# Two order changes in a gated attention and state-space kernel: g products ahead of q products, and the copies of the output stage's first two pairs of chunks

## The chip, the cores and the metric

The kernel runs on one core of one Trainium2 chip. The metric is device time in microseconds (us) for one execution, from 2048 input rows of 448 numbers to 2048 output rows of 448 numbers. Before the change the median of three runs was 168.16 us. The engines are named as the profile names them: PE multiplies matrices, PEld is its weight load, DVE and ACT are the two elementwise engines that can read PE's results, POOL is a third elementwise engine that works on on-chip memory only, SP and POOL issue the transfers.

## The reference

The output is `g*a + (1-g)*b`. `a` is linear attention with 16 heads of 28, `b` is a state-space convolution, `g` is one gate per row.

```python
phi = lambda t: jnp.where(t > 0, t + 1, jnp.exp(t)) + 1e-6
pq, pk = phi(q), phi(k)                       # q, k, v = x @ wqkv, split in heads
kv = jnp.einsum("bhsd,bhse->bhde", pk, v)
z = jnp.einsum("bhsd->bhd", pk)
num = jnp.einsum("bhqd,bhde->bhqe", pq, kv)
den = jnp.einsum("bhqd,bhd->bhq", pq, z)[..., None] + 1e-6
a = (num / den).transpose(0, 2, 1, 3).reshape(B, S, D) @ wo
g = _sigmoid((x * gate_w).sum(-1, keepdims=True))
y = jnp.fft.irfft(jnp.fft.rfft(u_t, 2 * L) * Kf[None], 2 * L)[:, :, :L]
b = y.transpose(0, 2, 1) + u * D_skip
out = g * a + (1 - g) * b
```

## The kernel before

The 2048 rows are 16 chunks of 128. Products need about full precision from a fast matmul type, so every operand is split in a high and a low part, and a product of two operands is three matmuls (high with high, low with high, high with low). A "product" below is one of these matmuls.

**First stage, the loop over chunks (times about 24 to 112 us).** For each chunk PE runs three groups in turn. `project` makes 11 products of 448 columns for the keys of the next chunk (tile `k`, or a tile named `v` in every other chunk), then 11 products of 450 columns for the queries of this chunk (tile `q`; the two extra columns are the gate). `do_g` then makes 11 products of 448 columns that add `x^T phi(k)` into four accumulators `g0` to `g3`: three each for `g0`, `g1`, `g2`, and two for `g3`, the first of which loads only 64 columns of weights. So 22 products, 11 of `g` and 11 of `k`, lie between two runs of `q`. In two places there is more between them: four small transposes (tile `p`, line 319) within chunk 5's `g`, and two products (line 449) after chunk 12's. While PE does this, ACT and DVE turn `k` and `q` into features and split them, POOL makes low parts and products for `b`, and transfers bring the next chunk of `x`.

The work on each engine stands in the order in which the program was written (`manual_schedule`); no scheduler moves it. A framework adds the waits between engines. It counts two reads of one PE result tile by different engines as a conflict as well, and lets the later one in the program wait for the earlier.

**Middle stage (about 112 to 121 us).** From the copies `gs` of the four accumulators PE makes the key-value blocks (line 755), ACT and DVE mask and split them, and PE multiplies them with `wo` to a combined matrix of four blocks (`m_products`, line 735; split by `m_high` on ACT, line 739, and `m_low` on DVE, line 743). The last chunk's `q` run is spread over this stage in pieces (`q_run`), to fill PE's waits.

**Output stage (about 117 to 163 us).** For a pair of chunks (even, odd) the steps are: `norm_a` (POOL, line 596) multiplies the query features with the key sums, `norm_b` (DVE reduction, line 601) sums them per head, `norm_d` (DVE, lines 605 and 607, and a copy to on-chip memory on ACT, line 610) makes the reciprocal, `norm_c` (POOL lines 621 and 628, DVE line 624) scales the features. `turn_pe` (PE, line 633) transposes them: four transposes for an even chunk, the last of which holds pieces of both chunks, and three for an odd one. `turn_even` copies the even chunk's result, high part on ACT (line 640), low part on DVE (line 641); `turn_odd` does the same for the odd chunk (ACT line 652, DVE line 659) with four small copies on ACT from the even chunk's result (`odd_ends`, line 656). `attend` (PE, line 676) makes 11 products of 448 columns for one chunk; its first takes a high part, its second a low part. `final_b` (DVE line 681) and `final_c` (ACT line 687) empty its result.

A pair's `attend` products are issued one chunk late: `turn_pe` of chunks 2 and 3 comes ahead of `attend(1)`, and `attend(2)` follows it.

Of the kernel before, what the change touches and what calls it, by code (L numbers as in the profile page):

```python
# [7 lines left out]
F32 = mybir.dt.float32  # L8
# [3 lines left out]
ALU = mybir.AluOpType  # L12
# [10 lines left out]
J = 4  # L23
# [11 lines left out]
PADS = 32  # L35
G = 4
ROWS = {6: (0, 1), 7: (2, 3, 4), 8: (5, 6, 7), 9: (8, 9, 10), 10: (11, 12, 13), 11: (14, 15)}
SMALL = 2.0 ** -70
FLAT = 2.0 ** 35
BIG = 3.4028234e38  # L40
# [102 lines left out]
def gated_mix_kernel(ctx: ExitStack, tc: tile.TileContext, xin, wq_d, wvo_d, abc_d, ldt_d, dsk_d,  # L143
                     turn_d, cst_d, first_d, gin_d, out):
    nc = tc.nc
    PE, ACT, DVE, POOL, SP = nc.tensor, nc.scalar, nc.vector, nc.gpsimd, nc.sync
# [62 lines left out]
    o = 0  # L209
    for part in PARTS:  # L210
# [8 lines left out]
        o = e  # L219
# [124 lines left out]
    def project(*args, **kw):  # L344
        o, run = pieces(*args, **kw)
        run(11)
        return o
# [57 lines left out]
    gp = gps.enter_context(tc.tile_pool(name="gp", bufs=1, space=PSUM))  # L405
    g = [gp.tile([P, 512], F32, name="g%d" % i, tag="g%d" % i) for i in range(4)]

    def do_g(c, blocks=range(4)):
        w = xn[c]
        for i in blocks:  # L410
            a = w[:, 64 + i * P:64 + (i + 1) * P]
            b = w[:, XC - NAT + 64 + i * P:][:, :P] if i < 3 else None
            seq = [(a, pkh[c]), (a, pkl[c]), (b, pkh[c])] if i < 3 else \
                  [(a, pkh[c]), (a[:, :64], pkl[c])][::1 if c == 0 else -1]
            for n, (a, b) in enumerate(seq):
                PE.matmul(g[i][:a.shape[1], :D], lhsT=a, rhs=b, start=c == 0 and n == 0,  # L416
                          stop=c == NC - 1 and n == len(seq) - 1)

# [7 lines left out]
    def home(c):  # L426
        return homes[c // (2 * G)][:, c % (2 * G)]

    def running(c):
        if not c:  # L430
            sums.append(ps.tile([P, 512], F32, name="r", tag="v0")[:, :D])
            ACT.copy(sums[0], home(0))
        else:
            DVE.tensor_tensor(out=sums[0], in0=home(c), in1=sums[0], op=ALU.add)
        DVE.tensor_tensor(out=home(c), in0=near, in1=sums[0], op=ALU.mult)
# [82 lines left out]
    for c in range(2, NC - 2):  # L518
        if c + 3 < NC:
            load_x(c + 3)  # L520
        if c == 2:
            SP.dma_start(out=mask, in_=cst_d)
        if c in (6, 7):
            half_load(1, c - 6)
        if c == 10:
            for j in (0, 2):
                SP.dma_start(out=wo[:, j:j + 2], in_=wvo_d[:DJ, 1, j:j + 2])
        if c == 12:
            for j in (0, 2):
                SP.dma_start(out=wv[:, j:j + 2], in_=wvo_d[:, 0, j:j + 2])  # L530
        ko = project(c + 1, wkh, wkl, D, "v1" if c in (2, 4) or c > 6 and c % 2 == 0 else "k")
        rows = list(ROWS.get(c, ()))
        if c > 6 and rows:
            running(rows.pop(0))
        if c == 13:
            under(room[:, G:G + 2])
            under(room[:, G + 2:])
        split_t(c + 2)
        if c == 13:
            ACT.copy(over, sums[0])  # L540
            head_add(0)
            head_add(1)
        if c > 5:
            split_n(c + 2, False)
        k_feature(c + 1, ko)
        if c in (8, 9, 11):
            group_add((c - 7) * 2 // 3)
        if c == 12:
            whole_split()
        if c > 5:  # L550
            skip(c + 2)
        k_high(c + 1)
        k_low(c + 1)
        if rows:
            running(rows.pop(0))
        qo = project(c, wqh, wql, D + 2, "q")
        q_post(c, qo)
        for i in rows:
            running(i)
        if c < 5:  # L560
            steps(2 if c == 4 else 1)
        if c == 4:
            ACT.copy(tri, trir)
        if c == 7:
            SP.dma_start(out=okr[:, None, :DJ], in_=oks[:, None, :])
        if c == 9:
            DVE.tensor_reduce(out=okr[:, DJ:], in_=okr[:, :DJ], op=ALU.add, axis=AX.X)
            DVE.tensor_copy(okn, okr[:, DJ:])
        do_g(c, (0, 1))
        if c == 5:  # L570
            steps(1)
        do_g(c, (2, 3))
        if c < 4:
            skip(c - 1)
            skip(c + 2)
        if c < 6:
            split_n(c + 2, c > 3)
        if c in (3, 4):
            half_load(0, c - 3)
        for j in {11: (0, 1), 12: (2, 3)}.get(c, ()):  # L580
            split_o(j)
        if c == 12:
            whole_head()
        if c == 13:
            group_add(3)
            under(y[:, 2 * G:2 * G + 2])
            under(y[:, 2 * G + 2:3 * G])
# [4 lines left out]
    pn, th, tl, pd, dn, dp = {}, {}, {}, {}, {}, []  # L592
# [10 lines left out]
    def norm_d(c, n, copy=DVE.tensor_copy):  # L603
        r = dp[0][:, c:c + n]
        DVE.scalar_tensor_tensor(out=r, in0=r, scalar=1e-6, in1=e1[:, c:c + n, None].to_broadcast([P, n, H]),
                                 op0=ALU.add, op1=ALU.mult)
        DVE.reciprocal(out=r, in_=r)
        if c % 2 == 0:
            dn[c // 2] = tp.tile([P, 4, H], F32, name="den", tag="den", bufs=3)
        copy(dn[c // 2][:, c % 2:c % 2 + n], r)  # L610
# [19 lines left out]
    def turn_pe(c):  # L630
        o = p3.tile([P, 512], F32, name="tr", tag="tr")
        for j in range(4 - c % 2):
            PE.transpose(o[:, j * P:(j + 1) * P], pn[c][:, j], ident)  # L633
        return o

    def turn_even(c, o):
        t = xt_p.tile([P, 2, J, P], F32R, name="th", tag="t")
        th[c], tl[c] = t[:, 0], t[:, 1]
        ov = o.rearrange("p (j t) -> p j t", j=J)
        ACT.copy(th[c], ov)  # L640
        DVE.tensor_tensor(out=tl[c], in0=ov, in1=th[c].bitcast(F32), op=ALU.subtract)  # L641

    def turn_odd(c, o, oe):
        odd_high(c, o)
        odd_ends(c, 0, oe)
        odd_ends(c, 1, oe)
        odd_low(c, o)

    def odd_high(c, o):
        t = xt_p.tile([P, 2, J, P], F32R, name="th", tag="t")  # L650
        th[c], tl[c] = t[:, 0], t[:, 1]
        ACT.copy(th[c][:, :3], o[:, :3 * P].rearrange("p (j t) -> p j t", j=3))

    def odd_ends(c, i, oe):
        for half in (slice(0, DT), slice(DT, P)):
            ACT.copy((th, tl)[i][c][half, 3], oe[i * DT:(i + 1) * DT, 3 * P:])  # L656

    def odd_low(c, o):
        DVE.tensor_tensor(out=tl[c][:, :3], in0=o[:, :3 * P].rearrange("p (j t) -> p j t", j=3),
                          in1=th[c][:, :3].bitcast(F32), op=ALU.subtract)  # L660
# [17 lines left out]
    def final_b(c):  # L678
        ot = tp.tile([P, D], F32, name="ot", tag="pkh")
        for a, lo, hi in av[c]:  # L680
            DVE.scalar_tensor_tensor(out=ot[:, lo:hi], in0=y[:, c, lo:hi], scalar=og[:, c:c + 1],  # L681
                                     in1=a[:, lo:hi], op0=ALU.mult, op1=ALU.add)
            (ACT if c == NC - 1 and hi == D else SP).dma_start(out=oview[c, :, lo:hi], in_=ot[:, lo:hi])
# [5 lines left out]
    c = NC - 2  # L689
# [7 lines left out]
    k_low(c + 1)  # L697
    zh = tp.tile([P, D], F32R, name="zh", tag="w")
    zl = tp.tile([P, D], F32R, name="zl", tag="v0", bufs=1)
    qo = project(c, wqh, wql, D + 2, "q")  # L700
    do_g(c, (0, 1, 2))
    zo = ps.tile([P, 512], F32, name="zo", tag="v0")
# [13 lines left out]
    for i in range(4):  # L716
        do_g(c + 1, (i,))
        ACT.copy(gs[i], g[i][:, :D])
        if i == 1:
            qo, q_run = pieces(c + 1, wqh, wql, D + 2, "q")  # L720
# [17 lines left out]
    def m_high(j, o):  # L738
        ACT.copy(mh[:DJ, j] if j < 3 else shl[:, 0], o[:DJ, :D])
# [34 lines left out]
    def kv_low(r, o):  # L774
        DVE.tensor_tensor(out=kvl[:, 2 * r:2 * r + 2], in0=o, in1=kvh[:, 2 * r:2 * r + 2].bitcast(F32), op=ALU.subtract)

    q_run(1)
    k1 = kv_products(1)
    k0 = kv_products(0)
    k1 = kv_split(1, k1)  # L780
# [16 lines left out]
    t0 = turn_pe(0)  # L797
    t1 = turn_pe(1)
    q_run(2)
    norm_a(4)  # L800
    turn_even(0, t0)
    odd_high(1, t1)
    norm_b(2)
    norm_b(3)
# [2 lines left out]
    o1 = m_products(1, ps, "v0")  # L807
    m_high(0, o0)
    m_high(1, o1)
    ACT.copy(mh[:DT, 3], shl[:DT, 0].bitcast(F32))  # L810
    odd_ends(1, 0, t0)
    norm_d(2, 2, ACT.copy)
    ACT.copy(low_w3[0][:DT], shl[:DT, 0].bitcast(F32))
    m_low(0, o0)
    m_low(1, o1)
# [25 lines left out]
    norm_b(4)  # L841
    norm_a(7)
    norm_b(5)
    norm_d(4, 2, ACT.copy)
    for c in range(2, NC, 2):
        more = c + 2 < NC
        final_b(c - 2)
        t0 = turn_pe(c)
        t1 = turn_pe(c + 1)
        if more:  # L850
            norm_c(c + 2)
        if c + 6 < NC:
            norm_a(c + 6)
        if c + 4 < NC:
            norm_b(c + 4)
        turn_even(c, t0)
        if more:
            norm_c(c + 3)
        if c + 6 < NC:
            norm_a(c + 7)  # L860
        turn_odd(c + 1, t1, t0)
        final_c(c - 2)
        attend(c - 1, ((0, D),))
        if c + 4 < NC:
            norm_b(c + 5)
            norm_d(c + 4, 2, ACT.copy)
        final_b(c - 1)
        final_c(c - 1)
        attend(c, ((0, D),))
        for _ in range({4: 1, 6: 2}.get(c, 0)):  # L870
            next(later, None)
# [92 lines left out]
```

## Time and profile before

| | us |
|---|---|
| median of 3 runs (168.1, 168.16, 168.77) | 168.16 |
| the profiled execution's own time | 168.38 |
| its span in the trace, first to last instruction | 166.4 |
| PE busy, share of the span | 161.1, 97% |
| DVE busy | 116.1, 70% |
| ACT busy | 109.4, 66% |
| POOL busy | 104.9, 63% |
| mean granted TensorE clock | 0.997 |

A row of the chain of waits has a start, a duration and what ran; the chain joins the pieces of work that set the end. A row of the timeline has the same, for all instructions of one engine, with the idle time before a row and who ended it in brackets. A duration of a single PE product in the timeline is its latency (about 0.36 us); what a product costs in a stream is the distance to the next one's start.

### The profile page before, as it was taken

Reading aid. Unit: us, or ns where it says so; the run is one execution under the profiler, and the core shown is the slowest. Engines: PE = TensorE matmul, PEld = TensorE weight load, DVE = VectorE, ACT = ScalarE, POOL = GpSimd, SP = SyncE. Lnnn points to the kernel's source line nnn. Section 1 sums busy time; section 2 is a strip of 40 time slices with the busy share of each in tenths; the row PEclk is TensorE's granted clock in tenths of the full one; section 3 lists DMA queues with packets and bytes.
Section 4 is the critical chain, followed back from the end, with each engine's and each line's share of the span. In section 5 each row is a group of like instructions: output and inputs, shape, how many; then the busy total and the mean of one; then the engine's idle time right before and its main releaser. Section 6 shows DMA issues by size and latency. Waiting matters only on the chain.

```text
span 166.4 us, 2609 instructions
## 1 busy us (share of the span) xinstructions
PE 161.1 (97%) x835; PEld 144.9 (87%) x835; DVE 116.1 (70%) x243; ACT 109.4 (66%) x257; POOL 104.9 (63%) x116
## 2 busy tenths in 40 slices
PE   6999999999999999999999999999999999999991
PEld 2698999999999999999999999988987999999990
DVE  0837753685852879889885555898899979986441
ACT  3688668988486784766758966453856766676541
POOL 3073589678809449477295999749689998633000
PEclk9999999999999999999999999999999999999998
DMA  5999966687974330959988007997121221122222
GB/s 157 411 314 321 287 143 230 228 295 276 336 255 136 126 107 19 221 141 250 295 261 165 0 4 117 185 203 161 27 46 55 110 110 55 61 110 110 110 78 95
DMA packets 10783, 27.51 MB, mean 165 GB/s; under 512 B 1328, under 2 KB 6992, under 8 KB 10544
## 3 DMA queue, kind: packets, MB, share of 16 engines
q1 hardware_dynamic: 8992, 21.71, 39.1%
q0 software_dynamic: 1632, 5.51, 17.6%
q8 instruction: 7, 0.11, 0.3%
q10 hardware_dynamic: 144, 0.11, 0.2%
q14 instruction: 8, 0.07, 0.1%
HBM read 17.87 MB, written 3.67 MB: 129 GB/s over the span
## 4 chain that ended last, share of the span: by engine, by line
PE 87%; DVE 6%; DMA 2%; ACT 1%; issue 1%; ACTq 0%; DVEq 0%
PE g L416 21%; PE q L340 19%; PE a L676 19%; PE v L340 12%; PE k L340 11%; PE tr L633 3%; DMA y<-in 2%; DVE den L601 2%; PE k L755 1%; DVE wk L743 1%; DVE th L641 1%; DVE ot L681 1%; ACT kvh L772 0%; DVE shl L743 0%; ACT wk L466 0%
## 5 line engine op out<-in xcount | busy, mean ns | idle before, releaser
L676 PE MATMUL a<-wk,th 128*128 128x448 f32 (+1 forms) x178 | 37.4, 357 | 0.3 <-DVE th L641 0.3
L416 PE MATMUL g<-pkh,xn 128*128 128x448 f32 x112 | 35.7, 364 | 0.0
L676 PEld LDWEIGHTS a<-wk,th 128*128 128x128 f32 x178 | 31.3, 188 | 2.9 <-DVE th L641 0.7
L237 POOL TENSOR_TENSOR xt<-xr,xt 128x512 fp32r<-128x512 f32 x14 | 18.2, 1298 | 19.8 <-ACT xt L241 19.8
L340 PE MATMUL q<-wqh,xt 128*128 128x450 f32 x120 | 27.8, 367 | 0.0
L237 POOL TENSOR_TENSOR xn<-xr,xn 128x448 fp32r<-128x448 f32 x16 | 19.6, 1228 | 10.1 <-ACT xn L247 10.1
L340 PEld LDWEIGHTS q<-wqh,xt 128*128 128x128 f32 x120 | 22.5, 189 | 1.8
L416 PE MATMUL g<-pkl,xn 128*128 128x448 f32 x64 | 23.3, 364 | 0.0
L416 PEld LDWEIGHTS g<-pkh,xn 128*128 128x128 f32 x112 | 21.1, 188 | 2.3
L596 POOL TENSOR_TENSOR prod<-pq,zb 128x448 f32<-128x448 f32 x16 | 18.3, 1154 | 4.5 <-ACT zb L709 2.9
L253 POOL TENSOR_TENSOR y<-xr,dsk 128x448 f32<-128x448 f32 x16 | 20.4, 1281 | 0.0
L340 PE MATMUL k<-wk,xt 128*128 128x448 f32 x88 | 19.7, 366 | 0.1
L340 PE MATMUL v<-wk,xt 128*128 128x448 f32 x88 | 18.9, 362 | 0.0
L340 PEld LDWEIGHTS k<-wk,xt 128*128 128x128 f32 x88 | 16.4, 188 | 2.0 <-ACT wk L466 0.5
L340 PEld LDWEIGHTS v<-wk,xt 128*128 128x128 f32 x88 | 16.5, 188 | 1.1
L681 DVE SCALAR_TENSOR_TENSOR ot<-y,og,a 128x448 f32<-128x448 f32 (+1 forms) x17 | 10.7, 626 | 7.5 <-PE a L676 7.3
L621 POOL TENSOR_TENSOR room<-pq,den 128x336 f32<-128x336 f32 x16 | 12.1, 756 | 5.4 <-issue 2.6
L687 ACT COPY pq<-a 128x448 f32<-128x448 f32 (+1 forms) x17 | 8.6, 512 | 5.8 <-DVE ot L681 5.6
L416 PEld LDWEIGHTS g<-pkl,xn 128*128 128x128 f32 x64 | 11.2, 174 | 1.1 <-DVE pkl L379 0.2
L656 ACT CAST th<-tr 64x128 fp32r<-64x128 f32 x32 | 8.3, 261 | 5.5 <-DVE th L641 5.1
L340 PE MATMUL q<-wql,xt 128*128 128x450 f32 x45 | 11.7, 366 | 0.0
L369 DVE SCALAR_TENSOR_TENSOR k<-k,e 128x448 f32<-128x448 f32 x8 | 5.1, 632 | 9.0 <-ACT e L368 8.8
(155 smaller groups left out, 289.7 us busy)
## 6 DMA issues: line engine op xcount, KB each, us to landing
xr<-in SPq DMA_DIRECT2D x15, 512.0 KB, 3.9
out<-ot SPq DMA_DIRECT2D x15, 224.0 KB, 1.9
room<-in SPq DMA_DIRECT2D x3, 896.0 KB, 7.5
wvo<-in SPq DMA_DIRECT2D x2, 896.0 KB, 5.5
y<-wvo POOLq DMA_DIRECT2D x2, 896.0 KB, 8.2
y<-room POOLq DMA_DIRECT2D x2, 896.0 KB, 9.2
y<-over POOLq DMA_DIRECT2D x2, 896.0 KB, 9.5
y<-in SPq DMA_DIRECT2D x2, 480.0 KB, 4.7
```

Source lines behind the costliest of these rows:

```text
L237: eng.tensor_tensor(out=o, in0=r, in1=h.bitcast(F32), op=ALU.subtract)
L253: POOL.tensor_tensor(out=y[:, c], in0=plain[c][:, :D], in1=dsk, op=ALU.mult)
L340: PE.matmul(o[:, :n], lhsT=a, rhs=b, start=run.n == 1, stop=not seq)
L369: DVE.scalar_tensor_tensor(out=pks[c], in0=pks[c], scalar=1.0, in1=e, op0=ALU.add, op1=ALU.max)
L416: PE.matmul(g[i][:a.shape[1], :D], lhsT=a, rhs=b, start=c == 0 and n == 0, stop=c == NC - 1 and n == len(seq) - 1)
L596: POOL.tensor_tensor(out=pd[c], in0=pq[:, c], in1=zb, op=ALU.mult)
L621: POOL.tensor_tensor(out=n[:, :3, :DJ].rearrange("p j (h d) -> p j h d", h=4), in0=a, in1=r[:, :H - 4].rearrange("p (j h) -> p j h", j=3)[ ...
L633: PE.transpose(o[:, j * P:(j + 1) * P], pn[c][:, j], ident)
L656: ACT.copy((th, tl)[i][c][half, 3], oe[i * DT:(i + 1) * DT, 3 * P:])
L676: PE.matmul(a[:, lo:hi], lhsT=u_, rhs=w_[:, lo:hi], start=n == 0, stop=n == 10)
L681: DVE.scalar_tensor_tensor(out=ot[:, lo:hi], in0=y[:, c, lo:hi], scalar=og[:, c:c + 1], in1=a[:, lo:hi], op0=ALU.mult, op1=ALU.add)
L687: ACT.copy(pq[:, c, lo:hi], a[:, lo:hi])
```

## The change

It moves instructions and removes or adds none; each engine executes the same operations. There are four edits.

1. A table `EARLY` gives, for nine chunks, how many of the three products of `g0` (none, one or two) are issued ahead of that chunk's `q` run in place of right behind it.
2. The first piece of the last chunk's `q` run in the middle stage has two products where it had one; the last piece has one fewer.
3. For the first pair (chunks 0 and 1) `norm_d` of chunks 2 and 3 comes ahead of three ACT copies, and the low part of chunk 0's transposed features (DVE) comes after this `norm_d` and after the first two small ACT copies of `odd_ends`; it came ahead of both.
4. For the second pair (chunks 2 and 3) the high parts come first, then `norm_d` of chunks 4 and 5, then the low part of chunk 2, all ahead of `final_b(0)` and of `norm_c` of chunks 4 and 5. The loop's later pairs are written in another order too, but on each engine their order stays.

The PE stream at chunks 6 and 7, before. `k` is the next chunk's key tile, `q` this chunk's query tile, `g_140` the accumulator `g0`, `pkh` and `pkl` the high and low key features, `xn` the chunk's rows.

```order
L340 MATMUL k<-wk_70,xt 128x448 x11
L340 MATMUL q<-wqh,xt 128x450 x8
L340 MATMUL q<-wql,xt 128x450 x3
L416 MATMUL g_140<-pkh,xn 128x448
L416 MATMUL g_140<-pkl,xn 128x448
L416 MATMUL g_140<-pkh,xn 128x448
```

The same place with the change (chunk 6 with two products ahead, then chunk 7 with one):

```order
L341 MATMUL k<-wk_70,xt 128x448 x11
L419 MATMUL g_140<-pkh,xn 128x448
L419 MATMUL g_140<-pkl,xn 128x448
L341 MATMUL q<-wqh,xt 128x450 x8
L341 MATMUL q<-wql,xt 128x450 x3
L419 MATMUL g_140<-pkh,xn 128x448
```

Two products of `g0` have moved from behind the `q` run to ahead of it. Counted over the loop, 24 or 21 products now lie between two runs of `q` where 22 did.

The DVE stream of the output stage's first pair, before. `wk` holds the combined matrix, `th` the transposed features, `den` the reciprocals.

```order
L743 TENSOR_TENSOR wk_70<-m_1270,wk_70 112x448
L641 TENSOR_TENSOR th<-tr,th 128x512
L601 TENSOR_REDUCE den<-prod 128x16 x2
L605 SCALAR_TENSOR_TENSOR den<-den,e_61 128x32
L607 RECIPROCAL den<-den 128x32
L743 TENSOR_TENSOR wk_70<-m_1304,wk_70 112x448
```

With the change:

```order
L747 TENSOR_TENSOR wk_70<-m_1271,wk_70 112x448
L605 TENSOR_REDUCE den<-prod 128x16 x2
L609 SCALAR_TENSOR_TENSOR den<-den,e_61 128x32
L611 RECIPROCAL den<-den 128x32
L650 TENSOR_TENSOR th<-tr,th 128x512
L747 TENSOR_TENSOR wk_70<-m_1304,wk_70 112x448
```

The low part of chunk 0 (`th`) has moved behind the reciprocal of chunks 2 and 3.

The ACT stream at the same place, before:

```order
L739 CAST wk_70<-m_1308 112x448
L810 CAST wk_70<-shl 64x448
L656 CAST th<-tr 64x128 x2
L610 COPY den<-den 128x32
L813 CAST wk_70<-shl 64x448
```

With the change:

```order
L743 CAST wk_70<-m_1308 112x448
L614 COPY den<-den 128x32
L815 CAST wk_70<-shl 64x448
L659 CAST th<-tr 64x128 x2
L818 CAST wk_70<-shl 64x448
```

The copy of the reciprocal has moved ahead of one matrix copy and of the first two small copies from chunk 0's transposed result.

The diff:

```diff
+EARLY = {3: 2, 4: 1, 6: 2, 7: 1, 9: 2, 10: 1, 12: 2, 13: 2, 14: 1}
...
-    def do_g(c, blocks=range(4)):
+    def do_g(c, blocks=range(4), part=None):
...
             for n, (a, b) in enumerate(seq):
+                if i == 0 and (n < EARLY.get(c, 0)) != (part == "early"):
+                    continue
                 PE.matmul(g[i][:a.shape[1], :D], lhsT=a, rhs=b, start=c == 0 and n == 0,
...
+        do_g(c, (0,), "early")
         qo = project(c, wqh, wql, D + 2, "q")
...
     def turn_even(c, o):
+        even_high(c, o)
+        even_low(c, o)
+
+    def even_high(c, o):
         t = xt_p.tile([P, 2, J, P], F32R, name="th", tag="t")
         th[c], tl[c] = t[:, 0], t[:, 1]
-        ov = o.rearrange("p (j t) -> p j t", j=J)
-        ACT.copy(th[c], ov)
-        DVE.tensor_tensor(out=tl[c], in0=ov, in1=th[c].bitcast(F32), op=ALU.subtract)
...
+        ACT.copy(th[c], o.rearrange("p (j t) -> p j t", j=J))
+
+    def even_low(c, o):
+        DVE.tensor_tensor(out=tl[c], in0=o.rearrange("p (j t) -> p j t", j=J), in1=th[c].bitcast(F32), op=ALU.subtract)
...
-    q_run(1)
+    q_run(2)
...
-    turn_even(0, t0)
+    even_high(0, t0)
     odd_high(1, t1)
     norm_b(2)
     norm_b(3)
...
     m_high(0, o0)
     m_high(1, o1)
+    norm_d(2, 2, ACT.copy)
     ACT.copy(mh[:DT, 3], shl[:DT, 0].bitcast(F32))
     odd_ends(1, 0, t0)
-    norm_d(2, 2, ACT.copy)
+    even_low(0, t0)
     ACT.copy(low_w3[0][:DT], shl[:DT, 0].bitcast(F32))
...
-    norm_d(4, 2, ACT.copy)
     for c in range(2, NC, 2):
         more = c + 2 < NC
-        final_b(c - 2)
         t0 = turn_pe(c)
         t1 = turn_pe(c + 1)
+        if c == 2:
+            even_high(c, t0)
+            odd_high(c + 1, t1)
+            norm_d(c + 2, 2, ACT.copy)
+            even_low(c, t0)
+        final_b(c - 2)
         if more:
             norm_c(c + 2)
+        if c == 2:
+            norm_c(c + 3)
...
-        turn_even(c, t0)
-        if more:
-            norm_c(c + 3)
+        if c > 2:
+            turn_even(c, t0)
+            odd_high(c + 1, t1)
+            if more:
+                norm_c(c + 3)
...
-        turn_odd(c + 1, t1, t0)
+        for i in range(2):
+            odd_ends(c + 1, i, t0)
+        odd_low(c + 1, t1)
```

More of the change, by code (lines that the diff above doesn't have):

```diff
@@ L636, in turn_even @@
     def turn_even(c, o):
+        even_high(c, o)
+        even_low(c, o)
+    def even_high(c, o):
         t = xt_p.tile([P, 2, J, P], F32R, name="th", tag="t")
         th[c], tl[c] = t[:, 0], t[:, 1]
-        ov = o.rearrange("p (j t) -> p j t", j=J)
-        ACT.copy(th[c], ov)
[L641 to L647, printed above, removed]
+        ACT.copy(th[c], o.rearrange("p (j t) -> p j t", j=J))
+    def even_low(c, o):
+        DVE.tensor_tensor(out=tl[c], in0=o.rearrange("p (j t) -> p j t", j=J), in1=th[c].bitcast(F32), op=ALU.subtract)
     def odd_high(c, o):
@@ L699, in gated_mix_kernel @@
     zl = tp.tile([P, D], F32R, name="zl", tag="v0", bufs=1)
+    do_g(c, (0,), "early")
     qo = project(c, wqh, wql, D + 2, "q")
```

## The prediction

> **What bounds the kernel now.** I read the page's head and its chain of waits by engine first, then the chain in order of time, then the timelines of PE, DVE and ACT where the chain leaves PE.
>
> ```profile
> PE 161.1 (97%) x835; PEld 144.9 (87%) x835; DVE 116.1 (70%) x243; ACT 109.4 (66%) x257; POOL 104.9 (63%) x116
> PE 87%; DVE 6%; DMA 2%; ACT 1%; issue 1%; ACTq 0%; DVEq 0%
> ```
>
> PE sets the end for 87% of the span and DVE for 6%. Two questions follow: what a PE product costs in the loop, and what DVE does where the chain is on it. The loop, from the chain in order of time (start, duration, what):
>
> ```profile
> 30.91 2.29 PE q L340 x11
> 44.22 2.27 PE q L340 x11
> 47.70 0.39 PE p L319 x4
> 51.31 2.20 PE q L340 x11
> 53.51 2.21 PE g L416 x11
> 55.72 2.20 PE k L340 x11
> 57.91 2.27 PE q L340 x11
> 60.19 2.22 PE g L416 x11
> ...
> 91.19 2.20 PE q L340 x11
> 95.60 0.41 PE v L449 x2
> 98.22 2.21 PE q L340 x11
> ...
> 104.83 2.27 PE q L340 x11
> ```
>
> The groups follow without gaps. A run of 11 products takes 2.20, 0.200 each, but a `q` run takes either 2.20 to 2.21 or 2.27 to 2.29 (0.206 each). The long ones are those of chunks 3, 5, 7, 9, 11 and 14, the short ones 4, 6, 8, 10, 12 and 13. With 22 products between two runs (11 `g`, 11 `k`) the kinds alternate. Where two products of line 449 make it 24, between chunks 12 and 13, a short run follows a short one. So a run's kind depends on how many products lie ahead of it, and 22 and 24 leave different remainders: with a period of two both would act alike, with a period of three 24 changes nothing and 22 moves on by one.
>
> Now the output stage's start on PE, then on DVE, then on ACT, from the timelines:
>
> ```profile
> 112.17 0.37 PE L340 MATMUL q<-wqh,xt 128*128 128x450 f32 x1
> 120.83 2.39 PE L676 MATMUL a<-wk,th 128*128 128x448 f32 x11
> 123.06 1.15 PE L633 MATMUL tr<-both,room 128*128 128x128 f32 x7
> 123.97 2.26 PE L676 MATMUL a<-wk,th 128*128 128x448 f32 x10
> 126.26 0.37 PE L676 MATMUL a<-wk,th 128*128 128x448 f32 x1
> 126.97 2.27 PE L676 MATMUL a<-wk,th 128*128 128x448 f32 x10 [0.34 <-DVE th L641]
> 129.08 0.93 PE L633 MATMUL tr<-both,room 128*128 128x128 f32 x7
> 129.76 1.06 PE L676 MATMUL a<-wk,th 128*128 128x448 f32 x4
> ```
>
> ```profile
> 118.03 0.61 DVE L743 TENSOR_TENSOR wk<-m,wk 112x448 fp32r<-112x448 f32 x1
> 118.56 0.68 DVE L641 TENSOR_TENSOR th<-tr,th 128x512 fp32r<-128x512 f32 x1
> 119.16 1.35 DVE L601 TENSOR_REDUCE den<-prod 128x16 f32<-128x448 f32 x2
> 120.78 0.37 DVE L607 RECIPROCAL den<-den 128x32 f32<-128x32 f32 x1
> 121.05 1.14 DVE L743 TENSOR_TENSOR wk<-m,wk 112x448 fp32r<-112x448 f32 x2
> 124.61 0.37 DVE L607 RECIPROCAL den<-den 128x32 f32<-128x32 f32 x1
> 126.24 0.68 DVE L641 TENSOR_TENSOR th<-tr,th 128x512 fp32r<-128x512 f32 x1
> ...
> 130.72 0.68 DVE L641 TENSOR_TENSOR th<-tr,th 128x512 fp32r<-128x512 f32 x1
> ```
>
> ```profile
> 119.21 1.14 ACT L739 CAST wk<-m 112x448 fp32r<-112x448 f32 x2 [0.38 <-PE m L735]
> 120.25 0.56 ACT L810 CAST wk<-shl 64x448 fp32r<-64x448 f32 x1
> 120.71 0.53 ACT L656 CAST th<-tr 64x128 fp32r<-64x128 f32 x2
> 121.27 0.19 ACT L610 COPY den<-den 128x32 f32<-128x32 f32 x1
> 121.35 0.57 ACT L813 CAST wk<-shl 64x448 fp32r<-64x448 f32 x1
> ```
>
> `attend(2)` starts at 126.26, and its second product, due at 126.46, waits until 126.97 for the low part of chunk 2 (DVE 126.24 to 126.92). The restart costs a little more: ten products to the next start at 129.08 take 2.11, not 2.00. The seven transposes at 123.06 take 0.91 to the next start, those at 129.08 take 0.68. Together some 0.84 is lost here (0.51 and 0.11 and 0.23).
>
> **Edit 1, g ahead of q.** Nothing is added; the early products wait for nothing, since the key features of a chunk are made one turn before its `q` run. A long `q` run costs 0.065 more than a short one, and the `g` run after it 2.22 for 2.205: 0.08 in all. The counts 24 and 21 are both multiples of three. Chunk 2's run is short, so by the period of three every later run is short. Six long runs go: 6 × 0.08 = 0.48. What may be given back: the half-loaded product of `g3` is reached at another point of the count, as it is after a long run; at worst that is 0.015 in eight chunks, 0.12, at best nothing. I take 0.05: **−0.43** (bounds −0.48 and −0.36 while the period holds; an unknown is the place with the transposes, below).
>
> **Edit 2, one more q product at 112.2.** It costs 0.20 there, and PE then waits for the copies of the accumulators anyway (row below, 0.2 of it on PEld alone). The 0.20 comes back at the end of the `q` run, ahead of `attend(0)` at 120.83. If the second product of `attend(0)` waits, as I find next, nothing is gained: **0** (bounds −0.20 and 0).
>
> ```profile
> PEld k L755 <- ACT gs L718: 0.2, 1, 0.2
> L656 ACT CAST th<-tr 64x128 fp32r<-64x128 f32 x32 | 8.3, 261 | 5.5 <-DVE th L641 5.1
> ```
>
> **Edit 3, the first pair.** The second of these rows decides. ACT's small copies read the same PE result as DVE's low part (both `th<-tr`), and nothing they need comes from that low part; still they have waited 5.1 us for it. They wait because they stand behind it in the program. With the change the first two stand ahead of it, so now DVE waits for ACT. Step by step:
>
> - DVE ends the matrix part at 118.64 and goes straight to the reductions, which start at 118.56 for 119.16 (rows overlap by 0.08): 0.60 earlier. The reciprocal ends at 121.15 − 0.60 = 120.55.
> - ACT is free at 120.35 (119.21 + 1.14), waits for the reciprocal, copies it from 120.58 to 120.77, and then needs, from the start of the line 810 copy, what it needed before from 120.25 to 121.24: 0.99. With the same overlap of 0.11 as between the rows 121.27 and 121.35 it starts at 120.66 and ends the two small copies at 121.65.
> - DVE has stood idle since 120.55. The low part of chunk 0 starts at 121.69 and ends at 122.37, where it ended at 119.24. Behind it on DVE stand the matrix parts of the first two blocks; they start at 122.29 for 121.05, end at 123.43, and are due later than the low part.
> - PE: `attend(0)` starts at 120.63 to 120.83 and its second product waits for that low part: 122.42 for 121.03. Ten products with a restart, 2.11: the transposes start at 124.53 for 123.06, **1.47 late**.
>
> What comes back: the reciprocal's copy is 0.69 earlier, so POOL is done before the transposes ask, and they take 0.68 for 0.91: `attend(1)` at 125.21 for 123.97, 1.24 late, and `attend(2)` at 125.21 + 2.29 = 127.50.
>
> **Edit 4, the second pair.** The low part of chunk 2 now follows the reciprocal at once. DVE does from 122.29 what it did from 121.05 to 124.98 (3.93), so it ends the reciprocal at 126.22 and the low part at 126.82; PE needs it at 127.70. The stall of 0.51 + 0.11 is gone, with 0.9 to spare. What is late next: `final_b(0)` stands behind that low part now, and its result tile is not written again before `attend(4)`. `attend(2)` ends 2.20 after its start, and the next transposes start at 129.70 for 129.08: **+0.62** for edits 2 to 4 together. PE is 0.62 late there and DVE 1.24. The low part of chunk 4 ended at 131.40 and was due at 129.76 + 2.29 + 0.20 = 132.25; now it ends by 132.64 and is due at 132.87, 0.2 to spare. From there PE runs without gaps as before. Bounds: −0.58 if the low part of chunk 0 doesn't wait for ACT (third rival), and +0.84 if only the transposes gain nothing.
>
> **Sum.** 168.38 − 0.43 + 0.62 = 168.57 against the profiled execution, which lies 0.22 above the median of the runs; against that median **168.4**.
>
> **The rivals.**
>
> *The count is lost at chunk 5* (slower). Four transposes of line 319 (0.39 at 47.70) lie between the runs of chunks 5 and 6. Before, a long run, 22 products and the four transposes were followed by a short one, as without them; that fits transposes that leave the count alone, and also ones that set it anew. If they set it anew, the two early products of chunk 6 move it off, its run is long, and by the rule 21 or 24 products after a long run never lead to a short one (22 do). Then chunks 6 to 14 are all long: 3 and 5 are saved (−0.16), 6, 8, 10, 12 and 13 are added (+0.40): +0.24 in place of −0.43, so 168.16 + 0.24 + 0.62 = 169.0.
>
> *The spacing has another cause.* One pair of runs carries the case of 24, none that of 21. If the kind follows the chunk's data or addresses, edit 1 is worth 0: 168.16 + 0.62 = 168.8. For it speaks the regular alternation; against it the break of the alternation at 13. The Trainium skill, "TensorE: Matmul & The Clock Gate", section "Back-to-back issue gap", has the isolated distance of two matmuls depend on the column count alone, N/2.4 + 2.5 ns, an estimate of 190 ns for 450 columns whatever stands ahead. By that rule edit 1 is worth nothing; the trace, with 200 and 206 ns for the same product, does not follow it.
>
> *The first pair does not stall* (faster). If DVE did the low part of chunk 0 right behind the reciprocal, it would end at 121.15 and PE's second product start at 121.20 for 121.03, 0.17 late; the transposes start 0.17 + 0.11 late, `attend(1)` 0.05, and with the 0.62 of `attend(2)` saved the stage is 0.57 to 0.58 earlier: 168.16 − 0.43 − 0.58 = 167.2. For it speaks that nothing but the order of two reads makes DVE wait; against it that ACT's copies have waited in just this way, in seven places. The Trainium skill, "PSUM — Partial Sum Buffer", section "Terms", counts two engines that read one bank at once as a collision, reads against reads included, so the wait is not idle caution.
>
> **How the numbers follow.** Forecast 0.40; count lost 0.19; other cause 0.18; no stall 0.18; 0.05 for a stall that I have not seen (later). What a measurement can tell from no change is 0.5%, 0.84 us: 167.3 to 169.0. The forecast and the other cause lie inside; no stall lies outside if edit 1 works as well; the count lost lies on the upper bound and goes two thirds to slower, with the 0.05. Faster 0.18, same 0.60, slower 0.22. The range, 167.1 to 169.2, takes in all four cases; the forecast's own is 168.2 to 168.7.
>
> **What would show it.** In the chain of waits `q` runs of 2.20 in all chunks from 2 to 14 (the rivals: 2.27 from chunk 6 on, or as before). On DVE a gap of about 1.15 ahead of the low part of chunk 0, ended by ACT's small copies; on PE a wait of some 1.5 behind the first product of `attend(0)`, seven transposes in 0.68 right after it, and no wait at `attend(2)`. The forecast is wrong if PE's wait at `attend(0)` is under half of that, if a granted clock below 1 follows it, or if DVE's delay makes a later `attend` wait.

## The result, and the profile after

The changed kernel took 169.47 us (median of 10 runs, 169.08 to 170.07), the kernel before 168.43 us beside it (168.03 to 169.4): ratio 1.0061 with a 95% interval of 1.0043 to 1.0079. The forecast was 168.4 with a range to 169.2. It is 1.04 us slower; the forecast was 0.2 us over the kernel before, too little to tell from no change.

The page of the changed kernel, busy times and the chain of waits by engine (span 167.8 us, the profiled execution's own time 169.69 us):

```profile
PE 161.2 (96%) x835; PEld 145.6 (87%) x835; DVE 115.9 (69%) x243; ACT 109.8 (65%) x257; POOL 105.1 (63%) x116
PE 92%; DVE 3%; ACT 2%; issue 0%; ACTq 0%; POOL 0%; DVEq 0%; POOLq 0%
```

PE is as busy as before and sets the end for more of the span. The chain in order of time shows the loop's `q` runs:

```profile
24.51 2.20 PE q L341 x11
31.52 2.21 PE q L341 x11
37.92 2.26 PE q L341 x11
44.39 2.27 PE q L341 x11
...
99.02 2.26 PE q L341 x11
105.48 2.26 PE q L341 x11
```

Chunks 2 and 3 are short as forecast. From chunk 4 on every run is long, the rows left out too: 11 long runs, where six were to become none. From the start of chunk 2's `q` run to the first product on `gs` (line 759, line 755 before) it took 88.69 us, 0.20 of it the added `q` product, for 88.24 before: 0.25 longer, not 0.43 shorter. This stretch is "the loop" in what follows, without the added product; it is taken between the products' own starts, which lie about 0.16 us ahead of those in the chain.

The output stage's start on PE, then on DVE, then on ACT, from the timelines:

```profile
121.08 0.43 PE L679 MATMUL a<-wk,th 128*128 128x448 f32 x1
122.87 2.28 PE L679 MATMUL a<-wk,th 128*128 128x448 f32 x10 [1.36 <-DVE th L650]
124.98 0.93 PE L637 MATMUL tr<-both,room 128*128 128x128 f32 x7
125.67 2.25 PE L679 MATMUL a<-wk,th 128*128 128x448 f32 x10
127.95 2.37 PE L679 MATMUL a<-wk,th 128*128 128x448 f32 x11
130.16 0.93 PE L637 MATMUL tr<-both,room 128*128 128x128 f32 x7
```

```profile
120.62 0.37 DVE L611 RECIPROCAL den<-den 128x32 f32<-128x32 f32 x1
122.12 0.69 DVE L650 TENSOR_TENSOR th<-tr,th 128x512 fp32r<-128x512 f32 x1 [1.14 <-ACT th L659]
126.57 0.67 DVE L650 TENSOR_TENSOR th<-tr,th 128x512 fp32r<-128x512 f32 x1
```

```profile
121.02 0.19 ACT L614 COPY den<-den 128x32 f32<-128x32 f32 x1 [0.21 <-DVE den L611]
121.10 0.56 ACT L815 CAST wk<-shl 64x448 fp32r<-64x448 f32 x1
121.56 0.53 ACT L659 CAST th<-tr 64x128 fp32r<-64x128 f32 x2
```

DVE stands idle for 1.14 us until ACT's two small copies are done, and PE waits behind the first product of `attend(0)`. The stall at `attend(2)` is gone: 11 products in a row from 127.95. From the first product of the `q` piece (112.17 before, 112.63 now) to the transposes ahead of `attend(3)` it takes 17.54 us for 16.91: 0.62 longer. This stretch is "the stage" in what follows. Behind that PE needs the same time as before, 33.75 us for 33.77 to the end of its last product. So 0.25 + 0.62 = 0.87 us are located. The rest of the difference lies ahead of chunk 2 and behind PE's last product, where the executions differ among themselves (the start of chunk 2's run lies between 23.76 and 24.54 us in the traces of this study).

### The profile page after: what moved, and what is told of

Read it like the earlier page. It is cut to its first block, busy times and chain, and to the rows that moved or that the text cites. A ratio compares the mean times of both kernels' runs of the same rounds, so it can differ in the third digit from the quotient of the medians.

```text
span 167.8 us, 2611 instructions
## 1 busy us (share of the span) xinstructions
PE 161.2 (96%) x835; PEld 145.6 (87%) x835; DVE 115.9 (69%) x243; ACT 109.8 (65%) x257; POOL 105.1 (63%) x116
## 4 chain that ended last, share of the span: by engine, by line
PE 92%; DVE 3%; ACT 2%; issue 0%; ACTq 0%; POOL 0%; DVEq 0%; POOLq 0%
PE a L679 21%; PE g L419 21%; PE q L341 19%; PE v L341 12%; PE k L341 11%; PE tr L637 3%; PE q L260 3%; PE k L759 1%; DVE den L605 1%; ACT kvh L776 0%; DVE th L650 0%; DVE wk L747 0%; DVE shl L747 0%; POOL warm L194 0%; ACT wk L815 0%
## 5 line engine op out<-in xcount | busy, mean ns | idle before, releaser
L341 PE MATMUL k<-wk,xt 128*128 128x448 f32 x88 | 20.3, 375 | 0.0
```

Of the source, the lines that this page charges most:

```text
L341: PE.matmul(o[:, :n], lhsT=a, rhs=b, start=run.n == 1, stop=not seq)
```

## The experiments

### One half of the change at a time

Edit 1 alone, with the output stage as before:

```diff
+EARLY = {3: 2, 4: 1, 6: 2, 7: 1, 9: 2, 10: 1, 12: 2, 13: 2, 14: 1}
...
+        do_g(c, (0,), "early")
         qo = project(c, wqh, wql, D + 2, "q")
```

> The kernel before with edit 1 alone (the table of early g products), output stage as before. Theory of the half-loaded product: the kind of a q run follows a count of period three, and the half-loaded product of g3 moves that count by one or not, by where it is met; with 9 products of g behind chunk 3's run it does not, so chunk 4's run and all later ones are long. Expected: q runs of chunks 2 and 3 of 2.20 us, those of chunks 4 to 14 of 2.26 to 2.27, from the start of chunk 2's run to the first product on the accumulators' copies 0.2 to 0.3 us more than before, time +0.15% (168.4 to 168.9 where before has 168.4). Rival, that the long runs of the changed kernel come with the output stage's edits: runs as forecast, all 2.20, 0.4 us less.

Measured: 168.98 us, ratio 1.0017 (0.9994 to 1.0039); here and below the ratio is to the kernel before, run beside it. The interval includes 1, so the time alone shows no loss; in the trace the loop is 0.25 us longer. The chain of waits:

```profile
31.71 2.21 PE q L341 x11
38.12 2.26 PE q L341 x11
44.58 2.27 PE q L341 x11
...
105.68 2.26 PE q L341 x11
```

The long runs come from edit 1 and need nothing of the output stage. They begin at chunk 4, two chunks ahead of the transposes on which the first rival rested.

Edits 2 to 4 alone:

```diff
-EARLY = {3: 2, 4: 1, 6: 2, 7: 1, 9: 2, 10: 1, 12: 2, 13: 2, 14: 1}
+EARLY = {}
```

> The changed kernel with an empty table: edits 2, 3 and 4 without edit 1. Theory: DVE's low part of chunk 0 waits for ACT's two small copies, PE waits some 1.6 us behind attend(0)'s first product, and some of that comes back: the transposes ahead of attend(3) start 0.6 us later than before, time +0.6 us (+0.35%). The q runs alternate as before. Rival, that edit 1 carries the loss: no difference to before.

Measured: 169.26 us, ratio 1.0034 (1.0013 to 1.0056). The `q` runs alternate. Chunk 3's waits for DVE, and behind it chunk 4's is long and chunk 5's short, the other way round than in the kernel before; from chunk 6 on they are as there. On PE, from the timeline:

```profile
120.20 0.44 PE L679 MATMUL a<-wk,th 128*128 128x448 f32 x1
122.00 2.28 PE L679 MATMUL a<-wk,th 128*128 128x448 f32 x10 [1.36 <-DVE th L650]
129.30 0.93 PE L637 MATMUL tr<-both,room 128*128 128x128 f32 x7
```

The stage takes 17.55 us for 16.91, +0.64, with the same wait as in the changed kernel. The two halves make 0.17% + 0.34%, 0.51%; the whole change, 0.61%, has that in its interval.

Edit 4 alone, the second pair of chunks:

```diff
+        if c == 2:
+            even_high(c, t0)
+            odd_high(c + 1, t1)
+            norm_d(c + 2, 2, ACT.copy)
+            even_low(c, t0)
+        final_b(c - 2)
```

> The kernel before with edit 4 alone: for chunks 2 and 3 the high parts, the reciprocal of chunks 4 and 5 and the low part of chunk 2 ahead of final_b(0). Theory: the first pair is undisturbed, the low part of chunk 2 is ready at about 125.7 where PE asks at 126.46, so the wait of 0.51 us and its restart of 0.11 go and nothing takes their place: -0.6 us (-0.35%). Rival, that this edit carries part of the loss (DVE then late for chunk 4's low part): no gain or a loss, and a wait ahead of attend(4).

Measured: 167.89 us, ratio 0.9962 (0.9943 to 0.9981). On PE, from the timeline:

```profile
121.22 2.38 PE L675 MATMUL a<-wk,th 128*128 128x448 f32 x11
126.64 2.38 PE L675 MATMUL a<-wk,th 128*128 128x448 f32 x11
128.85 0.93 PE L633 MATMUL tr<-both,room 128*128 128x128 f32 x7
```

No wait at `attend(0)` and none at `attend(2)`; the stage takes 16.29 us, −0.62. Edit 4 is worth what its stall cost, and with edits 2 and 3 beside it the gain becomes a loss of the same size.

### What in edit 3 makes the stall

The low part of chunk 0 stays behind the reciprocal; only its order against the small copies is turned back (edits 2 to 4, `EARLY` empty):

```diff
-    odd_ends(1, 0, t0)
     even_low(0, t0)
+    odd_ends(1, 0, t0)
```

> Edits 2 to 4 without edit 1, and the low part of chunk 0 on DVE written ahead of the last two of chunk 0's four small ACT copies' pair, so that the ACT copies wait for it again and not it for them; it still comes behind the reciprocal of chunks 2 and 3. Theory (the whole stall is DVE's wait behind ACT's two reads of the same result): the second product of attend(0) is late by about 0.17 us and not by 1.6, attend(2) has no wait, and from the first product of the q piece at 112 to the transposes ahead of attend(3) it takes about 16.3 us (before 16.91, with edits 2 to 4 as they were 17.54): -0.6, the time 0.9955 to 0.998 of the one before. Rival (it is the place behind the reciprocal that costs): the wait at attend(0) stays over 1 us, and the stage takes 17.3 or more, the time at or above the one before.

Measured: 168.01 us, ratio 0.9958 (0.9935 to 0.998). DVE, then PE, from the timelines:

```profile
120.34 0.37 DVE L611 RECIPROCAL den<-den 128x32 f32<-128x32 f32 x1
120.61 0.67 DVE L650 TENSOR_TENSOR th<-tr,th 128x512 fp32r<-128x512 f32 x1
```

```profile
120.80 2.82 PE L679 MATMUL a<-wk,th 128*128 128x448 f32 x11
126.44 2.38 PE L679 MATMUL a<-wk,th 128*128 128x448 f32 x11
128.65 0.93 PE L637 MATMUL tr<-both,room 128*128 128x128 f32 x7
```

The low part now follows the reciprocal without a gap, the second product of `attend(0)` is 0.14 us later than before (counted from the `q` piece), and the stage takes 16.30 us, −0.61. So the whole loss of edit 3 is the order of two reads of one PE result, and the place behind the reciprocal costs next to nothing.

### What sets the kind of a q run

The page and the chain give sums of runs. The distances between the starts of neighbouring PE products, taken from the traces in ns, show more. Here is what follows a short `q` run in four kernels, up to the next `q` run; the bracket marks the distance behind the half-loaded product of `g3`:

```
before, chunk 6
  g  199 205 200 198 202 200 198 202 200 [200] 200
  k  198 202 200 198 202 200 198 202 200 198 202
  q  201 206 208 205 208 206 207 206 208 205 208   long
changed, chunk 3 (9 g behind q, 1 ahead of the next)
  g  199 204 201 197 202 201 197 [202] 201
  v  197 202 201 197 202 201 197 202 201 197 202
  g  201
  q  198 203 206 207 206 207 206 208 206 207 206   long
two early products in every chunk, chunk 7
  g  199 205 200 198 201 201 198 [202] 200
  v  198 202 200 198 202 200 198 201 201 198 202
  g  200 198
  q  202 205 197 201 200 200 200 199 201 200 199   short
full load, chunk 6
  g  199 204 201 197 202 201 197 202 201 [197] 202
  k  200 198 202 201 196 203 201 197 201 202 197
  q  203 204 198 200 200 199 201 200 200 200 200   short
```

Products of 448 columns start in a cycle of three distances, about 198, 202 and 200 ns, apart from the first two behind a `q` run. A `q` run that starts behind a 198 is short; behind a 202 or a 200 it is long. In the kernel before, the half-loaded product follows a 200, and the cycle skips one place: 198 opens the `k` run where the full load has 200. Where it follows a 198 (the two kernels in the middle) the cycle runs on as if it were fully loaded. Four kernels test this.

First, the two products of `g3` exchanged in chunks 2 to 14, so that the half-loaded one ends the group:

```diff
-                  [(a, pkh[c]), (a[:, :64], pkl[c])][::1 if c == 0 else -1]
+                  [(a, pkh[c]), (a[:, :64], pkl[c])][::-1 if c in (1, NC - 1) else 1]
```

> The kernel before with one difference: in chunks 2 to 14 the two products of g3 change places, so the half-loaded one (64 columns of weights) is the last of a g run instead of the last but one. No product moves past a q run, 22 lie between two runs as before. Theory of the half-loaded product: it is now met one place later in the cycle of three and does not move the count after a short run, so the runs of chunks 3 to 5 and 7 to 14 are 2.20 us; chunk 6's, behind the transposes, is open, and after a long one the next is short again. Time -0.40 to -0.48 us (-0.25%). Rival, that only the number of products between the runs counts, or the chunk itself: long and short alternate as before, time the same.

Measured: 168.00 us, ratio 0.9954 (0.9934 to 0.9974); the loop 0.30 us shorter, still 22 products between the runs. The chain of waits:

```profile
31.14 2.27 PE q L340 x11
37.83 2.20 PE q L340 x11
44.43 2.21 PE q L340 x11
...
98.11 2.26 PE q L340 x11
104.78 2.21 PE q L340 x11
```

Chunks 4 to 12 are all short. Moving one product by one place ended the alternation. Chunks 3 and 13 are long, where the expectation had them short: chunk 3's run contains a wait for DVE, and chunk 13's comes behind the pair of line 449. The ratio is a gain of 0.78 us, at least 0.44 by its interval, so the 0.30 us of the loop don't explain all of it. The stage takes 16.92 us as before, and nothing else in the trace accounts for the rest.

Second, two early products in every chunk from 3 to 14, again 22 between runs:

```diff
+EARLY = {c: 2 for c in range(3, NC - 1)}
```

> Two products of g0 ahead of q in every chunk from 3 to 14: 22 products between two q runs as before, but the half-loaded product is met two places earlier behind the q run. Theory (place of the half-loaded product): it is met after another of the three spacings, so the alternation of q runs goes away: those of chunks 3 to 5 short, chunk 6 (four transposes) and chunk 13 (two products of line 449) open, the others all alike within each stretch; the loop 0.3 to 0.45 us shorter if alike means short. Rival (only the number of products between two q runs counts): 22 products give the alternation as before, six long runs, the time that of before.

Measured: 168.04 us, ratio 0.998 (0.9964 to 0.9995); the loop 0.36 us shorter. The chain of waits, chunks 5 to 7:

```profile
44.33 2.21 PE q L341 x11
51.35 2.27 PE q L341 x11
58.03 2.21 PE q L341 x11
```

All runs are short but chunk 6's, behind the four transposes.

Third, the kernel before with nothing moved and that one product loading all 128 columns:

```diff
-                  [(a, pkh[c]), (a[:, :64], pkl[c])][::1 if c == 0 else -1]
+                  [(a, pkh[c]), (a if 1 < c < NC - 1 else a[:, :64], pkl[c])][::1 if c == 0 else -1]
```

> The kernel before with one thing changed: the product of g3 that loads 64 columns of weights loads all 128 in chunks 2 to 14 (it adds the low-by-low term to the result, which the kernel leaves out). No order moves. Theory (a half-loaded product moves the cycle of three spacings, a fully loaded one never does): with 22 full products behind a short q run the next starts one step on in the cycle, still short; chunks 4 to 12 short, 3 and 13 open (a wait for DVE, the pair of line 449), no alternation, the loop about 0.3 us shorter, ratio 0.996 to 0.9985. Rival (only the number of products counts): the alternation stays, six long runs, ratio 1.

Measured: 168.24 us, ratio 0.9978 (0.9959 to 0.9998); the loop 0.36 us shorter. The chain of waits:

```profile
37.21 2.21 PE q L340 x11
43.82 2.21 PE q L340 x11
...
97.50 2.26 PE q L340 x11
```

Short up to chunk 12 (chunk 3's takes 2.22 us with its wait for DVE), long only behind the pair of line 449. In the kernel before, the weight load of 64 columns took 134 ns and those of 128 columns 188. The number of loaded columns of one product in 33 decides, and with it the number of result rows that the product writes, which the edit doubles too; the order is that of the kernel before. This is the plainest proof against the rival that the number of products alone counts.

Fourth, the same full load in the changed kernel:

> The changed kernel, all four edits, with the one product of g3 that loads 64 columns of weights loading all 128 in chunks 2 to 14 (it adds the low-by-low term, which the kernel leaves out). Theory (the half-loaded product spoiled edit 1's count): now 21 and 24 products that all count alike lie between two q runs, so chunks 3 to 12 are short as the forecast had it; 13 is open (the pair of line 449 ahead of it) and 14 with it. The loop to the first product on gs is 0.3 to 0.45 us shorter than before (the changed kernel: 0.25 longer); the output stage keeps its +0.62: the time is 1.001 to 1.002 of the one before, 0.6 us under the changed kernel. Rival (the early places cost by themselves, whatever the load): long runs from chunk 4 on, ratio 1.006 as the changed kernel.

Measured: 169.22 us, ratio 1.0052 (1.0031 to 1.0072); the loop 0.36 us longer, the stage +0.64. The chain of waits:

```profile
24.67 2.21 PE q L341 x11
31.68 2.26 PE q L341 x11
38.14 2.27 PE q L341 x11
```

Both expectations missed: chunk 3 is long at once. Mine was worked out badly. It kept the multiples of three of the prediction, while the run before had shown that 22 full products keep a short run short; in a cycle of three 21 and 24 then cannot. So the rule has to be put as: behind a short run the next is short if the products between, plus one where the half-loaded one skips a place, leave a remainder of one by three. It fits the stretches above: before 22 + 1 (long), the pair of line 449 before 24 + 1 (short), the changed kernel's chunk 3 24 + 1 (short) and chunk 4 21 + 0 (long), full load 22 + 0 (short) and 24 + 0 (long). It says nothing of a run with a wait in it (chunk 3) or behind the transposes, and one stretch does not fit: with two early products in every chunk, the pair of line 449 makes 24 + 0, and the run is short.

### The rule put to a forecast, and the best of both

A new table made by this rule, and the reads of edit 3 in their old order; the rest is the changed kernel. At the pair of line 449, which the rule does not fit, the table has two early products on both sides, as in the run where a short one followed.

```diff
-EARLY = {3: 2, 4: 1, 6: 2, 7: 1, 9: 2, 10: 1, 12: 2, 13: 2, 14: 1}
+EARLY = {3: 2, 4: 2, 5: 2, 6: 1, 8: 2, 9: 2, 10: 2, 11: 2, 12: 2, 13: 2, 14: 2}
...
-    odd_ends(1, 0, t0)
     even_low(0, t0)
+    odd_ends(1, 0, t0)
```

> The changed kernel with two things changed: the numbers of the table, and the low part of chunk 0 written ahead of the second pair of its small ACT copies. Theory, as corrected by the last run: a short q run is followed by a short one where the products between them, plus one if the half-loaded product of g3 is met at the ninth or tenth place behind the run (and not at the eighth or eleventh), make 22 or 25, never 21, 23 or 24; four transposes start the count anew, with 17 products from them to the run in place of 16 where the half-loaded product is met ahead of them or at their second place. The new table (two each for 3, 4, 5, then one for 6, none for 7, two each from 8 on) is made by this rule: all q runs from 2 to 14 are short (2.205), the loop 0.35 to 0.45 us shorter than before, the stage to the transposes ahead of attend(3) 0.6 shorter; ratio 0.9935 to 0.995, over 1.5 us under the changed kernel. Rival (the rule only fits the runs it was made from): long runs from chunk 6, 7 or 8 on, the loop at or above that of before, ratio 0.9965 to 0.999.

Measured: 167.56 us, ratio 0.9948 (0.9929 to 0.9966). The chain of waits, chunks 5, 6 and 14, then PE's timeline:

```profile
44.29 2.21 PE q L341 x11
51.12 2.21 PE q L341 x11
...
104.59 2.21 PE q L341 x11
```

```profile
119.98 2.83 PE L679 MATMUL a<-wk,th 128*128 128x448 f32 x11
127.83 0.93 PE L637 MATMUL tr<-both,room 128*128 128x128 f32 x7
```

All 13 runs are short, the loop is 0.42 us shorter, the stage takes 16.31 us, −0.60. By the two ratios this version is 1.1% under the changed kernel and 0.5% under the one before.

Another way to the same end, the half-loaded product last, three early products in chunk 3 and one in chunk 13, and edit 4 alone:

```diff
+EARLY = {3: 3, 13: 1}
...
-                  [(a, pkh[c]), (a[:, :64], pkl[c])][::1 if c == 0 else -1]
+                  [(a, pkh[c]), (a[:, :64], pkl[c])][::-1 if c in (1, NC - 1) else 1]
```

> The half-loaded product of g3 second of its two in chunks 2 to 14, so that every g group ends with it and the count is moved at one place only; three g0 products of chunk 3 and one of chunk 13 ahead of their q runs; and edit 4 alone of the output stage. Theory (spacings go in a cycle of three, and the half-loaded product moves the cycle by one only where it is met after two of the three): all q runs from 2 to 14 are short (2.205), the loop 0.45 to 0.5 us shorter than before, the stage to the transposes ahead of attend(3) 0.6 shorter: together -1.0 to -1.1, ratio 0.9935 to 0.995. If the gains of the two runs that had one each (0.9954 and 0.9962) just add, 0.992. Rival (the early products of chunks 3 and 13 set the cycle wrong): long runs from 13 on or from 3 on, ratio 0.996 to 0.998.

Measured: 167.46 us, ratio 0.9931 (0.9906 to 0.9956); all runs from chunk 2 to 14 are short, the loop 0.42 us shorter. In its profiled execution (169.13 us, the longest of the seven) a transfer came late; PE's timeline, and the row of the DMA issues:

```profile
124.32 0.64 PE L679 MATMUL a<-wk,th 128*128 128x448 f32 x2 [1.82 <-DMA wk<-shl]
```

```profile
wk<-shl SPq DMA_DIRECT2D x1, 112.0 KB, 4.3
```

Its output stage can't be read from that trace; the other six runs, 166.94 to 167.87, agree with both gains.

## Why the prediction was wrong, point by point

**Edit 1: wrong, and by this alone the sum.** Forecast −0.43 us, measured +0.25. The step that failed is the sentence on the half-loaded product: "is reached at another point of the count, as it is after a long run; at worst that is 0.015 in eight chunks". It priced the product in its own time and took the count as given. But that product is a part of the count: it adds one place where it follows a 200 or 202, none where it follows a 198. "The counts 24 and 21 are both multiples of three" was read from runs in which the product stood tenth behind `q` and added one each time; 24 + 1 and 21 + 1 keep a run short (chunks 3 of the changed kernel and 7 of the one with the new table), 24 + 0 and 21 + 0 do not (chunk 3 with full load in the changed kernel, chunk 4 of the changed kernel). The two early products of chunk 3 are no longer ahead of it, so it moves from the tenth place to the eighth, adds nothing, and chunk 4's run starts behind a 200. After that the rule that the first rival used, that 21 or 24 products after a long run never lead to a short one, held in every trace that has such a run, and all later runs stay long.

The price of a long run was about right: six fewer gave 0.42 us (0.48 forecast). Five more cost 0.25, less than 5 × 0.08, since chunk 3's long run before also held a wait for DVE and a run that starts behind a 200 takes 2.260 rather than 2.268, with `g` products of 0.201 behind it rather than 0.202.

**Edit 2: right.** `attend(0)` starts 0.21 us earlier, counted from the `q` piece, and the stall takes it back. No run has this edit alone.

**Edit 3: right to the hundredth.** Counted from the `q` piece, with the forecast behind: `attend(0)`'s second product 1.38 us late (1.39), the transposes 1.47 (1.47) in 0.68 us (0.68), `attend(1)` 1.25 (1.24). DVE's gap ahead of the low part is 1.14 (1.15).

**Edit 4: right.** No stall at `attend(2)`, edits 2 to 4 together +0.62 in the changed kernel (+0.62 forecast); −0.62 alone.

**The rivals.** *The count is lost at chunk 5* had the size, +0.24 for +0.25, by chance, and the wrong place: the count is off at chunk 4. But its premise holds: the transposes set the cycle anew. With 16 products between them and chunk 6's run this run is short whether chunk 5's was long (before) or short (edit 4 alone, edits 2 to 4 alone); with 18 it is long behind a long one (the changed kernel) and behind a short one (two early products in every chunk). So the table's two early products of chunk 6, which make it 18, would have ended the short runs there even if nothing had gone wrong at chunk 4. *The spacing has another cause* falls: a table made by the rule gave 13 short runs of 13. The estimate of 190 ns from the Trainium skill, "TensorE: Matmul & The Clock Gate", section "Back-to-back issue gap", is for an isolated product and is not what these products cost in their stream: the same 11 products of `q` take 2.205 to 2.269 us, by what stands ahead of them. *The first pair does not stall* was not the case here, and its working was sound: with the reads in their old order it came out as written, 0.14 us late (0.17) and −0.61 (−0.57 to −0.58).

Had edit 1's term been +0.25, the prediction's own sum would have been 168.16 + 0.25 + 0.62 = 169.0; with the kernel before at 168.43 beside the changed one it is 169.3, against 169.47 measured. The chances do not quite add up as written: two thirds of 0.19 with the 0.05 make 0.18 for slower, not 0.22.

**What stays open.** Why starts come in a cycle of three, why a run that starts behind a 198 keeps 200 ns, and why the half-loaded product skips a place is not shown by any run; nor is it shown whether its loaded columns or its result rows do it. How the pair of line 449 counts is not settled: as two in the kernel before, with full load and with the half-loaded product last, as three with two early products on both sides of it (in every chunk, and in the new table).

## What to carry to other kernels

When a product's cost depends on what stands ahead of it, list the start distances product by product before counting, and count every product of another shape, here a weight load of 64 columns, as something that may move the count. A rule read from places where such a product stood still says nothing on a change that moves it. Where two engines read one PE result, this framework lets the one written first go first: put the one that the next product waits for ahead.

## What the runs showed of the hardware that I had not expected

Eleven `q` products of one shape cost 2.205, 2.260 or 2.268 us by the phase in which they start, at a granted clock of 0.995 to 1.0 throughout, and one weight load of 64 columns in place of 128 can shift that phase for a dozen chunks.

The transfer of 112 KB from `shl` to `wk`, which lands in 2.2 us, took 4.3 and 3.9 us in two of the twelve profiled executions (the half-loaded product last with edit 4, and the kernel before with full load). PE then waited 1.82 and 1.38 us at `attend(0)`. What made it late is not shown.
